# Head pairs 4 and 5 of a planned attention and expert kernel: transposes and squares given to TensorE, bias table stored row by row, a buffer of its own for the first expert columns

## The chip, the cores and the metric

One core of one Trainium2 chip runs the whole program. The metric is device microseconds (us) of one execution. The kernel before takes 1083.62 us (median of three runs, 1081.85 to 1084.55). The profile is of a further execution, which took 1084.82 us by the same measure; its span from the first to the last instruction is 1083.0 us.

## The reference

```python
scores = scale * np.matmul(q, k.transpose(0, 1, 3, 2))      # B=4, H=8, S=576, D=64
x = (log1p(|i - j|) / log1p(max(i, 1)))[..., None]          # relative position
bias = np.maximum(x @ w1 + b1, 0.0) @ w2                    # hidden 32, one value per head
attn = softmax(scores + bias)                               # sum + 1e-9 below the line
x = concat_heads(attn @ v)                                  # (2304, 512)
h = np.maximum(np.maximum(x @ mw1, x @ mw2), x @ mw3) @ mwo # 512 -> 768 -> 512
gate = 1 / (1 + np.exp(-(h @ w_gate)))                      # 512 -> 1536
out = (gate * (h @ w_val)) @ w_out                          # 1536 -> 512, fp32
```

## The kernel before

**Numbers as pairs.** Most fp32 factors are split into a high and a low fp16 part, and a product is three fp16 matmuls (`mm3`, L914). The scale of a split comes from a sum of squares, which either ScalarE takes (`square_sum`, L581) or TensorE: five bf16 matmuls of the data with itself and a diagonal sum on VectorE (`square_sum_pe`, L593, L594).

**Attention.** Work goes by head pairs: P = 0 to 15, four to a batch. A pair has five steps, one for each tile of 128 query rows (the last has 64). A step (`pair`) loads its bias rows from the table `bias_d` (L815 on SP's queue or L816 on ACT's), makes the scores on PE (L804, L807), adds the bias with a row minimum on DVE (L820), takes the exponential on ACT (L821) and the reciprocal sum on DVE (L822, L823). The weights then have to be transposed, in one of two ways. `by_pe` scales them in fp32 on POOL (L831) or DVE (L832), transposes nine 128x128 blocks on PE (L836) and copies them out of PSUM (L574 on ACT, L575 on DVE). `by_dma` writes the high part on ACT (L844) and the low part on DVE (L845) and lets two DMA transposes (L847) move them. `value_out` (L863) multiplies with v: in fp32 (20 matmuls) after `by_pe`, in fp16 (30 matmuls, with v split by `v_hi` and `v_lo`, L785 and L789) after `by_dma`.

All 20 steps of batch 0 (pairs 0 to 3) go `by_pe`, tile by tile over the four pairs, between the rows of the bias table, which are made meanwhile (`bias_rows`, 36 times; each stores 16 table rows of all 8 heads, L661). In batches 1 to 3 the first two tiles of a pair go `by_pe` and the last three `by_dma`. While a pair runs, `prep` loads and splits q, k and v of the pairs to come; the squares of the first four pairs are on PE, those of all later ones on ACT.

**Experts.** `moe1` is the first expert layer of a batch (576 matmuls on L914: 36 column blocks of 12, first all of columns 0 to 255 and then the other 320, three weight matrices in turn for each, then 8 blocks of 18 with the fourth matrix). Its work of batch b-1 is recorded after the first pair of batch b. In batch 0 it keeps six column blocks at a time, three in `hm_f` and three in the end of the tile `X2`, from column 5760 on, and its sums go through two PSUM banks in turn (`mm_b`). The raw words of the fourth weight matrix (`mwo`) pass through two buffers in columns 3072 to 6144 of the same `X2`; their loads and decoding (L674, L536 to L538) are recorded before the first `moe1`. The second layer (`gate`, `outs`) follows at the end; it reuses the attention's memory.

**The planner.** All calls go into a `Recorder`, which notes what reads and writes which memory, and then puts the instructions of all engines into an order (`emit`). Each instruction has a class: BIAS before ATT before MOE before PREP. An engine takes the one that can start first by the planner's own costs, the higher class where two start together, and looks only so far ahead (72 instructions on PE). So the expert layers, class MOE, fill PE wherever the planner sees it idle. A call that has two engines to choose from, such as a copy out of PSUM, goes to the one that would end first. The order is fixed when the program is built; each engine then runs its list strictly in turn.

Of the kernel before, what the change touches and what calls it, by code (L numbers as in the profile page):

```python
# [121 lines left out]
class Recorder:  # L122
# [8 lines left out]
    def __init__(self, nc, untracked):  # L131
        self.nc = nc
        self.untracked = untracked
        self.items, self.first = [], 0
        self.mem = Mem()
        self.cls = 0
        self.joined = None
        self.t_eng = {e: 0.0 for e in self.WINDOW}
        self.busy = {e: 0.0 for e in self.WINDOW}
        self.t_dma = 0.0  # L140
        self.bank = {i: {} for i in range(8)}
        self.log = []
        self.passed = {e: False for e in self.WINDOW}
        for attr, eng in self.ENGINES.items():
            setattr(self, attr, Engine(self, getattr(nc, attr), eng))
# [52 lines left out]
    def cost(eng, method, out, reads, kwargs):  # L198
# [6 lines left out]
        if method.startswith("dma"):  # L205
            if "transpose" in method:
                return 1.33 if n > 1200 else 1.0 + 0.0003 * n, 0.12 + 0.00141 * n, 1.6
            dram = "DRAM" in str(out.space)
            if dram:
                n, parts = 1, 1  # L210
                for _, c in out.ap:
                    n *= c
            size = n * parts * (4 if "32" in str(out.dtype) else 2)
            return (0.45 if eng == "SP" else 0.1), size / (285e3 if dram else 400e3 if size > 6e5 else 300e3) * (1.6 if parts == 64 and n > 500 else 1.0) + 0.03, 1.85
        if eng == "PE":
            f32 = "float32" in str(reads[0].dtype)
            if method == "transpose":
                return 0.045 + 0.00055 * n, 0.0, 0.22
            if n <= 8:
                return 0.142, 0.0, 0.22  # L220
            t = (max(n / 2400, 0.03) + 0.0023) * (4 if f32 else 1)
            if kwargs.get("tile_position") is not None:
                depth = reads[0].ap[0][1]
                t *= (depth if depth < 128 else parts) / 128
                t += 0.012 if f32 else 0.008 if depth < 128 else 0.004
                if n <= 64:
                    t += 0.012
            return t, 0.0, 0.22
# [13 lines left out]
        t = {"tensor_tensor": 0.3 + 0.002 * n, "tensor_scalar": 0.08 + 0.00112 * n, "tensor_copy": 0.08 + 0.00112 * n}.get(method, 0.1 + 0.003 * n)  # L242
# [4 lines left out]
    def start(self, it, e):  # L247

        t = self.t_eng[e]
        for d in it.deps:  # L250
            e2, lat, own = self.ends[d]
            x = own if e2 == e == "PE" else lat
            if x > t:
                t = x
        for i in it.banks:
            for o, x in self.bank[i].items():
                if o != e and x > t:
                    t = x
        return t
# [33 lines left out]
    def emit(self):  # L293
# [15 lines left out]
        while left:  # L309
# [11 lines left out]
            if work:  # L321
                self.t_dma = max(self.t_dma, s + 0.3) + work
                f = self.t_dma + lat
                self.ends[it.k] = (None, f, f)
            else:
                self.ends[it.k] = (e, s + busy + lat, s + busy)
                for i in it.banks:
                    self.bank[i][e] = s + busy + lat
# [8 lines left out]
            stale |= {o for o in lists if self.passed[o] or picks[o] and (len(picks[o][1].alts) > 1 or picks[o][1].banks & it.banks)}  # L337
# [69 lines left out]
SIDE_CLS = ATT  # L407
TI1, T2 = 12, (24, 32, 36, 36, 36)
# [29 lines left out]
def tile_kernel(ctx, tc, q, k, v, w1, b1, w2, mw1, mw2, mw3, mwo, gw, vw, ow, xtab, masks, out):  # L438
# [17 lines left out]
    bias_d = dram.tile([H, S, SB], F32, tag="bias_d", name="bias_d")  # L456
# [46 lines left out]
    e_r = ring(Am, 2, 2 * S)  # L503
    PT0 = take(Am, 2304)
    PT1 = take(Am, 2880)
    pt0 = PT0.rearrange("p (t s) -> p t s", t=9)
    pt1 = [PT1[:, 1440 * e:1440 * (e + 1)].bitcast(F16).rearrange("p (t s) -> p t s", t=9) for e in range(2)]
    rvb0 = PT1[:, 0:2560].rearrange("p (h t d) -> p h t d", h=H, t=NIT)
# [133 lines left out]
    def bias_rows(ti):  # L642
# [18 lines left out]
        nc.sync.dma_start(bias_d[:, 16 * ti:16 * ti + 16, :].rearrange("h i j -> i h j"), bsb[:, 0:SB])  # L661
# [68 lines left out]
    def qk_squares(P, j):  # L730
        if j == 0:
            qs_t[P] = tiny_ap(2)
        (square_sum if P >= PPB else square_sum_pe)(rqk[:, j].rearrange("p h t d -> p (h t d)"), qs_t[P][:, j:j + 1])
# [35 lines left out]
    def v_squares(b, j):  # L769
        if j == 0:  # L770
            vs_t[b] = tiny_ap(PPB)
        (square_sum if b else square_sum_pe)(raw_v(b)[:, 2 * j:2 * j + 2].rearrange("p h t d -> p (h t d)"), vs_t[b][:, j:j + 1])
# [36 lines left out]
    def pair(P, it):  # L809
# [3 lines left out]
        src = bass.AP(tensor=bias_d.tensor, offset=(h0 * S + 128 * it) * SB + 64, ap=[[SB, m], [S * SB - 64, 2], [1, S]])  # L813
# [57 lines left out]
    def prep(u):  # L871
# [3 lines left out]
        if PPB <= P < NP:  # L875
            if P % PPB == 0 and s == 2:
                v_scales(b)
            if s == 5:
                v_hi(P)
            if s == 6:  # L880
                v_lo(P)
        Pl, s2 = divmod(u, 10)
        if 0 <= Pl < NP - PPB and s2 == 8:
# [45 lines left out]
    def moe1(b, xd, mm):  # L929
# [28 lines left out]
        if b == 0:  # L958
            mm_0 = [mm, mm]
            hms = [t[:, 320 * i:320 * (i + 1)] for t in (hm_f, X2[:, 5760:6912]) for i in range(3)]  # L960
# [87 lines left out]
    for b in range(1, B):  # L1048
        for P in range(PPB * b, PPB * b + PPB):
            for it in range(NIT):  # L1050
                m, (e, r) = rows[it], pair(P, it)
                if it < 2:
                    by_pe(e, r, m, pt0[:, :, 128 * it:128 * it + m])
                else:
# [8 lines left out]
            value_out(P, 256, 320, vb, pt1, False)  # L1063
# [178 lines left out]
```

## Time and profile before

| | |
|---|---|
| three runs, median (lowest to highest) | 1083.62 us (1081.85 to 1084.55) |
| profiled execution, its own time | 1084.82 us |
| its span, first to last instruction | 1083.0 us |
| PE busy / DVE / ACT / POOL | 1019.7 / 635.3 / 552.3 / 130.3 us |
| mean granted TensorE clock | 0.979 |

A page of the profile gives the busy time of each engine (part 1) and the span in 40 slices of 27 us (part 2: tenths of a slice; PEclk in tenths of the full 2.4 GHz). The timeline lists instructions in order, runs of equal ones merged (xN); a row's us reaches to the end of its last matmul, so the pace of a run is read from the start of one row to the start of the next. A bracket at the end of a row is idle time before it and what ended it.

### The profile page before, as it was taken

Reading aid. Unit: us, or ns where it says so; the run is one execution under the profiler, and the core shown is the slowest. Engines: PE = TensorE matmul, PEld = TensorE weight load, DVE = VectorE, ACT = ScalarE, POOL = GpSimd, SP = SyncE. Lnnn points to the kernel's source line nnn. Section 1 sums busy time; section 2 is a strip of 40 time slices with the busy share of each in tenths; the row PEclk is TensorE's granted clock in tenths of the full one; section 3 lists DMA queues with packets and bytes.
Section 4 is the critical chain, followed back from the end, with each engine's and each line's share of the span. In section 5 each row is a group of like instructions: output and inputs, shape, how many; then the busy total and the mean of one; then the engine's idle time right before and its main releaser. Section 6 shows DMA issues by size and latency. Waiting matters only on the chain.

```text
span 1083.0 us, 20927 instructions
## 1 busy us (share of the span) xinstructions
PE 1019.7 (94%) x8232; PEld 685.9 (63%) x8232; DVE 635.3 (59%) x1576; ACT 552.3 (51%) x1159; POOL 130.3 (12%) x159
## 2 busy tenths in 40 slices
PE   5877897799999999999999999999999999999998
PEld 2343465466566666676678777777765666776643
DVE  5866887788787887878899947922221221212210
ACT  6877896678788877777666426522110111211100
POOL 1011223503120422211110000000000000000000
PEclk9989898889999999999999999999999999999999
DMA  7767675978998989969855421000000000000001
GB/s 224 210 202 232 209 221 167 246 162 197 228 232 184 234 220 203 206 136 237 160 162 156 154 81 40 20 2 1 10 11 21 19 10 10 11 11 10 11 20 39
DMA packets 181133, 132.96 MB, mean 123 GB/s; under 512 B 123308, under 2 KB 152236, under 8 KB 181036
## 3 DMA queue, kind: packets, MB, share of 16 engines
q1 hardware_dynamic: 177364, 124.26, 46.0%
q10 hardware_dynamic: 3672, 7.38, 2.3%
q8 instruction: 64, 1.05, 0.4%
q14 instruction: 33, 0.27, 0.1%
HBM read 89.53 MB, written 16.52 MB: 98 GB/s over the span
## 4 chain that ended last, share of the span: by engine, by line
PE 79%; DVE 8%; DMA 6%; ACT 4%; issue 2%; POOL 1%; SPq 0%; ACTq 0%; POOLq 0%; DVEq 0%
PE ps L914 46%; PE ps L1179 13%; PE ps L863 6%; PE ps L804 4%; PE ps L836 4%; PE ps L650 2%; DMA bias_d<-am 2%; PE ps L807 2%; DMA am<-in_q_dram 1%; DVE am L820 1%; ACT am L574 1%; POOL am L831 1%; DMA am<-am 1%; PE ps L548 1%; DVE wm L944 1%
## 5 line engine op out<-in xcount | busy, mean ns | idle before, releaser
L914 PE MATMUL ps<-wm 128*128 128x320 f16 (+2 forms) x2304 | 305.1, 286 | 3.3 <-DVE wm L944 2.9
L914 PEld LDWEIGHTS <-am 128*128 128x128 f16 x2304 | 225.5, 98 | 58.8
L914 PEld LDWEIGHTS <-wm 128*128 128x128 f16 x2304 | 222.8, 99 | 60.3 <-issue 8.8
L914 PE MATMUL ps<-x,am 128*128 128x288 f16 x1728 | 214.3, 286 | 0.0
L821 ACT ACTIVATE am<-am,small 128x576 f32<-128x576 f32 (+1 forms) x160 | 123.0, 770 | 43.9 <-DVE small L820 37.7
L1179 PE MATMUL ps<-wm 128*128 128x512 f16 x648 | 142.0, 379 | 0.0
L1153 DVE SCALAR_TENSOR_TENSOR wm<-ps,wm 128x576 f32<-128x576 f32 x48 | 36.4, 757 | 161.6 <-PE ps L914 160.4
L820 DVE CUSTOM_DVE_ANT_0 am<-ps,am 128x576 f32<-128x576 f32 (+1 forms) x160 | 117.6, 748 | 22.4 <-issue 5.5
L1150 ACT ACTIVATE wm<-ps,ug 128x576 f32<-128x576 f32 x48 | 35.6, 741 | 155.0 <-PE ps L914 154.8
L1179 PEld LDWEIGHTS <-wm 128*128 128x128 f16 x648 | 63.4, 98 | 74.0
L1154 ACT CAST wm<-wm 128x576 f16<-128x576 f32 x48 | 32.2, 671 | 129.4 <-DVE wm L1153 129.4
L863 PE MATMUL ps<-am 128*64 128x320 f16 (+3 forms) x1000 | 88.4, 323 | 6.9 <-DVE small L594 4.5
L831 POOL TENSOR_SCALAR am<-am,small 128x576 f32<-128x576 f32 (+1 forms) x73 | 70.2, 971 | 198.1 <-DVE small L823 118.5
L836 PE MATMUL ps<-ident,am 128*128 128x128 f32 x396 | 66.5, 290 | 11.1 <-POOL am L831 7.5
L914 PE MATMUL ps<-am 128*128 128x288 f16 x576 | 71.2, 286 | 0.0
L574 ACT ACTIVATE am<-ps 128x512 f32<-128x512 f32 (+3 forms) x128 | 58.5, 473 | 15.3 <-PE ps L836 13.8
L1184 DVE TENSOR_TENSOR am<-ps,uo 128x512 f32<-128x512 f32 x16 | 11.1, 692 | 93.3 <-PE ps L1179 93.3
L845 DVE SCALAR_TENSOR_TENSOR am<-am,small 128x576 f16<-128x576 f32 (+1 forms) x72 | 59.2, 847 | 10.3 <-ACT am L844 9.7
L836 PEld LDWEIGHTS ps<-ident,am 128*128 128x128 f32 x396 | 45.7, 146 | 28.2 <-POOL am L831 15.3
L804 PE MATMUL ps<-am 64*128 64x512 f16 (+1 forms) x390 | 57.0, 389 | 3.2 <-DVE small L820 3.1
L581 ACT ACTIVATE junk<-am 128x640 bf16<-128x640 f32 (+1 forms) x72 | 48.8, 678 | 20.2 <-DVE am L538 8.9
L863 PEld LDWEIGHTS ps<-am 128*64 128x64 f32 x640 | 41.9, 150 | 22.7 <-issue 8.9
(148 smaller groups left out, 1181.1 us busy)
## 6 DMA issues: line engine op xcount, KB each, us to landing
am<-bias_d SPq DMA_DIRECT2D x52, 576.0 KB, 4.4
bias_d<-am SPq DMA_DIRECT2D x36, 320.0 KB, 3.5
wm<-in_moe_w_dram SPq DMA_DIRECT2D x12, 768.0 KB, 5.5
am<-bias_d ACTq DMA_DIRECT2D x12, 576.0 KB, 4.4
am<-in_moe_w_gate_dram SPq DMA_DIRECT2D x12, 512.0 KB, 4.6
am<-in_moe_w_val_dram SPq DMA_DIRECT2D x12, 512.0 KB, 4.6
am<-in_moe_w_out_dram SPq DMA_DIRECT2D x12, 512.0 KB, 3.4
out_dram<-am SPq DMA_DIRECT2D x36, 128.0 KB, 2.3
```

The costliest lines, as they stand in the source:

```text
L574: nc.scalar.activation(dst, src, AF.Copy, scale=scale)
L581: nc.scalar.activation(junk[:, 0:n], src, AF.Square, accum_out=acc)
L804: nc.tensor.matmul(s_main[o][:m], lhsT=q_[h, eq], rhs=k_[h, ek, 0:512], start=(i == 0), stop=(i == 2), tile_position=(64 * o, 0))
L820: nc.vector.tensor_tensor_reduce(e[:m, c], S_[o][:m], bt[:m, c], -1.0, 3.0e38, ALU.add, ALU.min, mx[:m])
L821: nc.scalar.activation(e[:m, c], e[:m, c], AF.Exp, scale=-1.0, bias=mx[:m], accum_out=l[:m, o:o + 1])
L831: nc.gpsimd.tensor_scalar(e[:m, c], e[:m, c], r[:m, o:o + 1], 1.0, op0=ALU.mult, op1=ALU.mult)
L836: nc.tensor.transpose(ps[:, t], e[:, 128 * (t0 + t):128 * (t0 + t) + 128], ident)
L845: nc.vector.scalar_tensor_tensor(ph[:m, 1, c], e[:m, c], f, ph[:m, 0, c], op0=ALU.mult, op1=ALU.subtract)
L863: nc.tensor.matmul(ps[64 * o:64 * o + 64, :N], lhsT=vv[:, o, tv], rhs=pp[:, tb], start=(i == j == 0), stop=(i == len(todo) - 1 and j == 4) ...
L914: nc.tensor.matmul(ps, lhsT=W(wp, kk), rhs=X(xp, kk), start=(first and i == 0), stop=(last and i == 2))
L1153: nc.vector.scalar_tensor_tensor(hm3(sg), pv, DOWN2, hm3(sg), op0=ALU.mult, op1=ALU.mult)
L1179: nc.tensor.matmul(po, lhsT=gT[:, gi, kk, 128 * ct:128 * ct + 128], rhs=OW[:, wi, kk], start=(kk == 0 and i == 0), stop=(kk == K2 - 1 and ...
```

## The change

1. **Pairs 4 and 5 whole by PE** (`PE_ALL = 6`). Their tiles 2, 3 and 4 go `by_pe` into an fp32 view of the same memory (`pt1_f`), and their second `value_out` is in fp32 from the raw v. `v_hi` and `v_lo` fall away for them, and the loads of the next batch's v into the same places come two substeps later (`prep`).
2. **Squares of batch 1 on PE** (`PE_SQ = 8`): q and k of pairs 4 to 7 and v of batch 1, twelve in all, through the PSUM region `sq_w`.
3. **The bias table as [row, head, column]** instead of [head, row, column]. A store of 16 rows is then one piece of DRAM, and a load reads 128 pieces of 4608 bytes (two heads side by side) instead of 256 of 2304.
4. **A buffer of its own** (`hm_x`, 960 columns of `Am`) for the three expert column blocks of batch 0 that were in `X2`.
5. **The planner's costs**: dearer DMA transposes, DMA issues on SP, POOL scalings and tiled matmuls; and a DMA may not be placed before the one eight places earlier has landed (`lanes`).

```diff
@@ class Recorder
+        self.lanes = [0.0] * 8
...
-                return 1.33 if n > 1200 else 1.0 + 0.0003 * n, 0.12 + 0.00141 * n, 1.6
+                return (1.55 if n > 1200 else 1.1 + 0.0003 * n), 0.12 + 0.00141 * n, 1.6
...
-        t = {"tensor_tensor": 0.3 + 0.002 * n, "tensor_scalar": 0.08 + 0.00112 * n, ...
+        t = {"tensor_tensor": 0.3 + 0.002 * n, "tensor_scalar": 0.09 + 0.0014 * n, ...
...
+        if it.alts[e][1][1]:
+            t = max(t, self.lanes[0])
...
+                self.lanes = self.lanes[1:] + [f]
@@ tables and buffers
+PE_ALL, PE_SQ = 6, 8
-    bias_d = dram.tile([H, S, SB], F32, tag="bias_d", name="bias_d")
+    bias_d = dram.tile([S, H, SB], F32, tag="bias_d", name="bias_d")
+    hm_x = take(Am, 960)
+    pt1_f = PT1.rearrange("p (t s) -> p t s", t=9)
@@ bias_rows
-        nc.sync.dma_start(bias_d[:, 16 * ti:16 * ti + 16, :].rearrange("h i j -> i h j"), bsb[:, 0:SB])
+        nc.sync.dma_start(bias_d[16 * ti:16 * ti + 16].rearrange("i h j -> (i h) j"), bsb[:, 0:SB])
@@ qk_squares (v_squares alike, with PPB * b + j < PE_SQ)
-        (square_sum if P >= PPB else square_sum_pe)(rqk[:, j].rearrange("p h t d -> p (h t d)"), qs_t[P][:, j:j + 1])
+        x, acc = rqk[:, j].rearrange("p h t d -> p (h t d)"), qs_t[P][:, j:j + 1]
+        if P < PE_SQ:
+            square_sum_pe(x, acc, sq_w if P >= PPB else sq_q)
+        else:
+            square_sum(x, acc)
@@ pair
-        src = bass.AP(tensor=bias_d.tensor, offset=(h0 * S + 128 * it) * SB + 64, ap=[[SB, m], [S * SB - 64, 2], [1, S]])
+        src = bass.AP(tensor=bias_d.tensor, offset=(128 * it * H + h0) * SB + 64, ap=[[H * SB, m], [SB - 64, 2], [1, S]])
@@ prep
-            if s == 5:
+            if s == 5 and P >= PE_ALL:
                 v_hi(P)
-            if s == 6:
+            if s == 6 and P >= PE_ALL:
                 v_lo(P)
         Pl, s2 = divmod(u, 10)
-        if 0 <= Pl < NP - PPB and s2 == 8:
+        if s2 == 0 and PPB <= Pl - 1 < PE_ALL:
+            Pl -= 1
+        elif s2 != 8 or PPB <= Pl < PE_ALL:
+            Pl = NP
+        if Pl < NP - PPB:
             load_v(Pl // PPB + 1, Pl % PPB)
@@ moe1
-            hms = [t[:, 320 * i:320 * (i + 1)] for t in (hm_f, X2[:, 5760:6912]) for i in range(3)]
+            hms = [t[:, 320 * i:320 * (i + 1)] for t in (hm_f, hm_x) for i in range(3)]
@@ batches 1 to 3
                 if it < 2:
                     by_pe(e, r, m, pt0[:, :, 128 * it:128 * it + m])
+                elif P < PE_ALL:
+                    by_pe(e, r, m, pt1_f[:, :, 128 * (it - 2):128 * (it - 2) + m])
                 else:
                     by_dma(e, r, m, pt1, 128 * (it - 2))
...
-            value_out(P, 256, 320, vb, pt1, False)
+            value_out(P, 256, 320, vb, pt1_f if P < PE_ALL else pt1, P < PE_ALL)
```

The changed program's line numbers are higher: L574 becomes L581, L581 becomes L588, L593 L600, L815 L830, L820 L835, L821 L836, L831 L846, L832 L847, L836 L851, L847 L862, L863 L878, L868 and L869 L883 and L884, L914 L933, L944 L963.

**ACT in batch 0.** ACT's list of before, in the fourth tile of batch 0: exponentials (L821), copies of transposes (L574 am<-ps), weight splits (L684) and squares of batch 1 (L581 on am 128x640).

```order
L684 ACTIVATE wm<-wm,small 128x768
L821 ACTIVATE am,small<-am,small 128x576
L868 ACTIVATE wm<-ps,small 128x128
L821 ACTIVATE am,small<-am,small 128x576
L581 ACTIVATE junk,small<-am 128x640
L574 ACTIVATE am<-ps 128x512
L581 ACTIVATE junk,small<-am 128x640
L821 ACTIVATE am,small<-am,small 128x576
```

The same tile in ACT's list of the changed program; L581 on am<-ps,small 128x256 is the copy of a finished expert column block into `hm_x`.

```order
L581 ACTIVATE am<-ps 128x128
L581 ACTIVATE am<-ps 128x512
L581 ACTIVATE am<-ps,small 128x256
L836 ACTIVATE am,small<-am,small 128x576
L691 ACTIVATE wm<-wm,small 128x768
L581 ACTIVATE am<-ps 128x512
L883 ACTIVATE wm<-ps,small 128x128
L581 ACTIVATE am<-ps 128x128
L836 ACTIVATE am,small<-am,small 128x576
L581 ACTIVATE am<-ps 128x512
L581 ACTIVATE am<-ps,small 128x256
```

The squares are gone from this place, and copies of expert blocks stand between the exponentials of batch 0. In the list of before the next such copies come 50 rows further on, in the first pair of batch 1 (x_71 is the tile `X2`):

```order
L581 ACTIVATE junk,small<-am 128x640
L574 ACTIVATE am<-ps 128x4x128
L574 ACTIVATE x_71<-ps,small 128x256 x2
L844 ACTIVATE am<-am,small 128x576
L581 ACTIVATE junk,small<-x_71 128x768
```

There the two copies into `X2` stand behind a square of q and among the squares of the fourth weight matrix.

**DVE at the end of batch 0.** The changed program's list in the fifth tile of batch 0 (L963 takes the maximum with an expert column block, L884 on 128x64 is a value product of that tile, L692 splits the third weight matrix); in the list of before the first L944 after this tile stands 30 rows later, in pair 4.

```order
L963 SCALAR_TENSOR_TENSOR wm<-ps,small,wm 128x256
L692 SCALAR_TENSOR_TENSOR wm<-wm,small 128x768 x2
L963 SCALAR_TENSOR_TENSOR am<-ps,small,am 128x256
L692 SCALAR_TENSOR_TENSOR wm<-wm,small 128x768
L884 SCALAR_TENSOR_TENSOR wm<-ps,small,wm 128x64
```

So the second of the three expert matrices is worked on before batch 0 is over.

**SP in pair 4.** SP's list of before (L847 transposes weights, L764 q and k of a later pair):

```order
L815 DMA am<-bias_d 128x2x576 x2
L847 DMA_TRANSPOSE am<-am 128x9x128
L815 DMA am<-bias_d 128x2x576
L847 DMA_TRANSPOSE am<-am 128x9x128
L847 DMA_TRANSPOSE am<-am 128x9x64 x2
L815 DMA am<-bias_d 128x2x576
```

and of the changed program, at the same place:

```order
L775 DMA_TRANSPOSE am<-am 128x10x128
L830 DMA am<-bias_d 128x1152 x2
L714 DMA am<-in_q_dram 128x2x256
L716 DMA am<-in_q_dram 64x2x64
L775 DMA_TRANSPOSE am<-am 128x10x128
L731 DMA am<-in_v_dram 128x2x256
```

Between the bias loads of these pairs stand only loads and the transposes of q and k; the first L862 comes in pair 6.

## Rows read from the trace of the kernel before

**Rows 1.** The page: busy time, then PE in 40 slices

```profile
PE 1019.7 (94%) x8232; PEld 685.9 (63%) x8232; DVE 635.3 (59%) x1576; ACT 552.3 (51%) x1159; POOL 130.3 (12%) x159
...
PE   5877897799999999999999999999999999999998
```

**Rows 2.** Windows: stretch, length, busy us of each engine, PEclk, DMA, GB/s

```profile
0.00:160.00 160.00, 125.79 (x1273) 66.00 (x1275) 114.87 (x304) 122.92 (x251) 26.14 (x39) 0.94 0.73 218
...
140.00:160.00 20.00, 19.96 (x225) 13.38 (x226) 17.08 (x46) 17.88 (x43) 4.73 (x5) 1.00 0.74 241
...
160.00:226.00 66.00, 50.00 (x406) 31.00 (x402) 51.44 (x144) 43.58 (x109) 25.08 (x25) 0.82 0.68 179
226.00:540.00 314.00, 308.08 (x2672) 210.90 (x2670) 255.59 (x664) 239.87 (x537) 71.22 (x90) 1.00 0.92 205
540.00:672.00 132.00, 129.46 (x1070) 102.20 (x1070) 106.45 (x273) 70.72 (x152) 7.89 (x5) 1.00 0.39 119
```

**Rows 3.** Timeline of PE where the expert matmuls stop and start again

```profile
157.43 0.51 PE L593 MATMUL ps<-wm 128*128 128x128 bf16 x6
157.77 1.14 PE L914 MATMUL ps<-wm 128*128 128x256 f16 x9
...
162.16 0.49 PE L914 MATMUL ps<-wm 128*128 128x256 f16 x3
...
226.05 1.48 PE L914 MATMUL ps<-wm 128*128 128x256 f16 x12
...
227.51 7.69 PE L914 MATMUL ps<-wm 128*128 128x256 f16 x69
...
236.59 9.01 PE L914 MATMUL ps<-wm 128*128 128x256 f16 x78
```

**Rows 4.** Timelines of DVE and ACT at 219 to 221 us

```profile
219.18 1.80 DVE L538 SCALAR_TENSOR_TENSOR x<-x 128x768 int32<-128x768 int32 x2
...
218.89 0.74 ACT L581 ACTIVATE junk<-am 128x640 bf16<-128x640 f32 x1 [1.36 <-DMA am<-in_q_dram]
...
220.15 0.84 ACT L574 ACTIVATE x<-ps,small 128x256 f32<-128x256 f32 x2
```

**Rows 5.** The chain that ended last, 150 to 300 us: start, us, what

```profile
169.86 7.77 DMA wm<-in_moe_w_dram
...
212.40 6.38 DMA am<-in_q_dram
```

**Rows 6.** Timeline of PE in pair 4 and the start of pair 5

```profile
246.56 2.23 PE L863 MATMUL ps<-am 128*64 128x320 f16 x30
248.72 0.77 PE L836 MATMUL ps<-ident,am 128*128 128x128 f32 x5
249.41 0.82 PE L804 MATMUL ps<-am 64*128 64x512 f16 x6
...
257.38 2.38 PE L863 MATMUL ps<-am 128*64 128x256 f32 x20
259.69 0.62 PE L804 MATMUL ps<-am 64*64 64x512 f16 x4
```

**Rows 7.** Groups by line and shape, whole span: busy us, mean ns, idle before

```profile
L831 POOL TENSOR_SCALAR am<-am,small 128x576 f32<-128x576 f32 x66 | 61.2, 936 | 184.5 <-DVE small L823 114.1 <-PE ps L807 30.5 <-ACT am L574 9.7
...
L844 ACT ACTIVATE am<-am,small 128x576 f16<-128x576 f32 x48 | 35.2, 766 | 0.9 <-ACT am L821 0.5 <-DVE small L823 0.4
...
L581 ACT ACTIVATE junk<-am 128x640 bf16<-128x640 f32 x36 | 26.3, 729 | 2.5 <-DMA am<-in_q_dram 1.4 <-DMA am<-in_v_dram 0.8 <-issue 0.2
...
L944 DVE SCALAR_TENSOR_TENSOR wm<-ps,small,wm 128x256 f32<-128x256 f32 x42 | 20.1, 479 | 3.4 <-PE ps L914 2.8
...
L832 DVE TENSOR_SCALAR am<-am,small 128x576 f32<-128x576 f32 x14 | 7.5, 539 | 0.4
```

**Rows 8.** Groups on PE by line and shape, 226 to 640 us

```profile
L836 PE MATMUL ps<-ident,am 128*128 128x128 f32 x198 | 31.4, 278 | 1.1 <-POOL am L831 1.0
```

**Rows 9.** DMA issues of the bias table: KB each, us to landing

```profile
am<-bias_d SPq DMA_DIRECT2D x52, 576.0 KB, 4.4
```

More of the change, by code (lines that the diff above doesn't have):

```diff
@@ L213, in cost @@
             size = n * parts * (4 if "32" in str(out.dtype) else 2)
-            return (0.45 if eng == "SP" else 0.1), size / (285e3 if dram else 400e3 if size > 6e5 else 300e3) * (1.6 if parts == 64 and n > 500 else 1.0) + 0.03, 1.85
+            return (0.55 if eng == "SP" else 0.1), size / (285e3 if dram else 400e3 if size > 6e5 else 300e3) * (1.6 if parts == 64 and n > 500 else 1.0) + 0.03, 1.85
         if eng == "PE":
@@ L224, in cost @@
                 t *= (depth if depth < 128 else parts) / 128
-                t += 0.012 if f32 else 0.008 if depth < 128 else 0.004
+                t += 0.012 if f32 else 0.012 if depth < 128 else 0.006
                 if n <= 64:
@@ L241, in cost @@
             return t + (0.09 if "accum_out" in kwargs and vec else 0.01), 0.0, 0.14
-        t = {"tensor_tensor": 0.3 + 0.002 * n, "tensor_scalar": 0.08 + 0.00112 * n, "tensor_copy": 0.08 + 0.00112 * n}.get(method, 0.1 + 0.003 * n)
+        t = {"tensor_tensor": 0.3 + 0.002 * n, "tensor_scalar": 0.09 + 0.0014 * n, "tensor_copy": 0.09 + 0.0014 * n}.get(method, 0.1 + 0.003 * n)
         if method == "tensor_scalar" and kwargs.get("op1") == ALU.max:
@@ L336, in emit @@
                     stale |= set(u.alts)
-            stale |= {o for o in lists if self.passed[o] or picks[o] and (len(picks[o][1].alts) > 1 or picks[o][1].banks & it.banks)}
+            stale |= {o for o in lists if self.passed[o] or picks[o] and (len(picks[o][1].alts) > 1 or picks[o][1].banks & it.banks or work and picks[o][1].alts[o][1][1])}
             for o, ks in lists.items():
@@ L771, in v_squares @@
             vs_t[b] = tiny_ap(PPB)
-        (square_sum if b else square_sum_pe)(raw_v(b)[:, 2 * j:2 * j + 2].rearrange("p h t d -> p (h t d)"), vs_t[b][:, j:j + 1])
+        x, acc = raw_v(b)[:, 2 * j:2 * j + 2].rearrange("p h t d -> p (h t d)"), vs_t[b][:, j:j + 1]
+        if PPB * b + j < PE_SQ:
+            square_sum_pe(x, acc, sq_w if b else sq_q)
+        else:
+            square_sum(x, acc)
     def v_scales(b):
```

## The prediction

> **What bounds the kernel now.** I read the page first: PE is busy for 1019.7 of 1083.0 us, and its slices read 9 from the tenth on [rows 1]. So the windows come next, cut where PE changes character [rows 2]. From 226 us on PE idles 6 us in 314, then 2.5 in 132, at a clock of 1.00; whatever stands there is paid in PE work, since the expert layer fills what the attention leaves. Before 226 us it is different: 34 us idle up to 160 us, and from 160 to 226 us 16 us idle with a mean clock of 0.82. The clock's two levels are 1.2 and 2.4 GHz, so 0.82 means about 36% of the 66 us at the lower one, 12 us of PE time lost (of which some 9 fell on busy time, busy being 50 of 66). That stretch, the last two tiles of batch 0, is the one place with PE time to win: about 25 us.
>
> Why is it empty, when expert work is there to fill it? The timeline of PE shows L914 stopping at 162.16 us and coming back at 226.05 us, with a run of 69, and then of 78 [rows 3]. In the order of PE 60 matmuls stand before the stop: five blocks of 12 of the first matrix. Blocks four and five must go to the part of `X2` that the raw words of the fourth matrix also pass through. On ACT both copies, `x<-ps,small`, stand at 220.15 us, behind the square of q and just after DVE starts its last two decodes `x<-x` (219.18 us) [rows 4]. From 162 to 220 us the two finished blocks hold the only two PSUM banks that `moe1` has, and no further one can begin. So the stop is a shared buffer, not a lack of work, and not the weights either: the first matrix is used by then, and the copies that PE waits for are not of weights.
>
> **The change part by part.**
>
> *The buffer (gain).* With `hm_x` the copies wait for no decode. I counted L914 in both orders ahead of the 25th step's scores, the last before the return at 226.05 us: 60 before, 252 now. The 192 matmuls that move up cost 192 x 0.115 us = 22.1 us at the pace of [rows 3] (78 in 9.01 us, at full clock). That is below the 25 us the stretch has. But PE, DVE and ACT run strictly in order, and the moved work brings its evacuations: by the orders, DVE gets 18 more maxima and splits ahead of that point at about 0.48 us (L944, [rows 7]), 8.6 us in a stretch where it is busy 51.4 of 66. The attention steps there wait on each other more than on an engine's total, so part of this lengthens the stretch. Bounds: it lengthens by nothing (gain 22 us), or by all of 8.6 us plus as much again for matmuls in front of attention work (gain 5 us). I take 4 us, nearer to the first since DVE has 14.6 us free there and a PE kept busy also runs that stretch's own matmuls at the higher clock: gain 18 us.
>
> *Two pairs by PE (cost).* Six steps, nine transposes each: 54. Five take 0.69 us from the first to the scores behind them [rows 6], 0.138 us each: 7.5 us. Two second value products change form: 30 fp16 matmuls take 2.16 us (246.56 to 248.72), 20 fp32 ones of 256 columns 2.31 us (257.38 to 259.69) [rows 6], so 2.31 x 320/256 = 2.89 us at 320 columns; +0.73 us each, 1.5 us. This lies after 226 us, where PE has no idle time: 9.0 us, all of it paid. In return ACT loses 12 casts of 766 ns and DVE as many subtractions, SP loses 12 transposes, and ACT or DVE get 18 copies out of PSUM; none of these bounds that stretch (DVE 256 and ACT 240 of 314 us [rows 2]), so their balance counts nothing, and it comes to a few us in any case.
>
> *Squares by PE (cost).* Twelve times five matmuls at 0.34 us for six, from 157.43 to 157.77 us [rows 3]: 3.4 us. By the order 35 of the 60 come before the 21st step, where PE has idle time; the other 25 are paid: 1.4 us. ACT loses 12 x (0.73 + 0.19 for reading the sum) us, in a stretch where it is busy three quarters. The wait moves with the square: ACT waited 1.4 us for q and 0.8 us for v over 36 squares [rows 7]. On PE such a wait holds all matmuls behind it, so I count 1 us more. Bounds: 0, and the one long case on the chain, a q load of 6.38 us [rows 5], for several of the twelve.
>
> *The bias table (nothing).* 4.4 us from issue to landing [rows 9] with three buffers ahead. Half as many pieces of twice the length move the same bytes. The trace has no piece of this length at this stride: a load could land 1 us sooner or 2 us later, and up to 226 us the DMA engines are busy about 0.7 of the time [rows 2]. Loads issued a step ahead hide either; if the cover went, DVE would wait at L820 for some of the 20 steps of batch 0. I take 0, with 3 us either way.
>
> *The planner's costs (nothing, with a spread).* POOL's scalings become dearer, and by the orders 25 more go to DVE in all: 539 ns there against 936 on POOL [rows 7], shorter for the step that waits, more work for DVE. Six of them lie before the 17th step. Other DMAs are issued later. After 226 us PE has only 6 us of idle time to lose or win; before 160 us the orders hold the same bias rows and steps in nearly the same place (96 and 116 of 144 bias products before the 7th and the 10th step now, 88 and 120 before). I take 0, with 4 us either way.
>
> The sum: -18 + 9.0 + 1.4 + 1 = -6.6 us against the profiled execution's 1084.8 us (1083.0 of span and 1.8 around it): 1078.2. The median of the runs is 1.2 us below that execution, so 1077.0 us.
>
> The Trainium skill speaks against the second part. Here 198 fp32 transposes ran between 226 and 640 us [rows 8], and the clock from 226 to 540 us was 1.00 [rows 2], with expert matmuls around them. "TensorE: Matmul & The Clock Gate", in "Part 4: PE-mode transpose", says that transposes do not count as activity for the clock in the way that matmuls do. By the rows the sum stays; by the page a pair transposed whole could fall to the lower clock, which is a rival below.
>
> **The rivals.**
>
> *Full recovery.* The stretch does not grow, its own matmuls run at the higher clock, and the start gains a little from ACT's lost squares. For it: from 140 to 160 us, where expert work was there, PE was busy 19.96 of 20 us at a clock of 1.00 [rows 2]. Then -25 + 11.4 and 1 us at the start: 1069 us. Against it: DVE's added work.
>
> *Given back.* The moved matmuls stand in front of attention work one for one and batch 0 ends about 10 us later: -12 + 11.4: 1083 us, no change. For it: steps there hang on single releases of DVE, POOL and PE; against it: 16 of the 66 us PE has nothing to do at all.
>
> *PE stands at the loads (slower).* PE now takes squares of q, k and v of pairs 4 to 7 in its strict order, and q's load waits for the one buffer of the pair before. A load took 6.38 us on the chain, and a weight load 7.77 us [rows 5]. If a third of the twelve squares find their load 4 us away, that is 16 us: -18 + 10.4 + 16 = +8, 1092 us. From 7.6 us of such waits on it is slower than before. Against it: ACT met only 2.2 us in 36, and the planner's `lanes` place DMAs later, so it expects landings later too.
>
> *The lower clock.* Two pairs transposed whole take about ten steps, some 50 us. At the 0.82 of [rows 2] they lose 18%, 9 us: 1086 us. By the page named above this is how it would go; the rows of 226 to 540 us stand against it.
>
> *The change does not do what it says:* the copies into `hm_x` could meet another late buffer. In the order they stand between exponentials of batch 0, so little is left for this; it would leave only the cost, 1095 us, and I put it with the slower case.
>
> **How the numbers follow.** Forecast, around 1077 (1071 to 1082): 0.51. Full recovery: 0.17. Given back: 0.16. PE at the loads, with the buffer that does not help: 0.13. Lower clock: 0.03. A measurement can tell 0.3%, 3.3 us, from no change: faster means under 1080.4, slower over 1086.9. Of the forecast 0.47 is faster and 0.04 the same; full recovery is faster (0.17); given back is the same but for 0.02 on each side; the lower clock and the stalls are slower, less 0.02 that ends as the same. Faster 0.66, same 0.18, slower 0.16. The range of 8 in 10 reaches from the full recovery to just past no change: 1066 to 1087 us.
>
> **What would show it.** The expert matmuls on PE (L933 now) should run on through 160 to 226 us, with copies `am<-ps,small` on ACT there; PE's idle time in that stretch should fall from 16 us to about 6, and its clock rise above 0.9. The scores of the 41st step, the first of batch 2, should stand 5 to 10 us earlier in the span. No DMA transposes of weights until pair 6. L851 should have 450 transposes of the same pace, and PE's busy time after batch 0 should be about 10 us more than what was moved out. I would be wrong in kind if PE shows waits of several us at L600 or at transposes for DMA, if batch 0 ends more than 8 us later, or if the time from the 25th step to the end of batch 3 grows.

## The result and the profile after

The changed kernel takes 1047.19 us (median of four runs, 1041.05 to 1053.29) against 1084.09 us before: 0.9654, interval 0.9581 to 0.9728. Six more runs of it gave 1044.44 us, 0.9637 (0.9609 to 0.9665). That is 37 to 39 us faster; 7 were forecast, and 1047 lies far below the range. The direction was right, the sum was not.

The page of the profiled execution (its own time 1053.29 us, span 1051.5, clock 0.991): busy time, then PE in 40 slices.

```profile
PE 1014.2 (96%) x8326; PEld 687.3 (65%) x8326; DVE 636.0 (60%) x1613; ACT 543.2 (52%) x1142; POOL 114.5 (11%) x141
...
PE   5798998999999899999999999999999999999998
```

Its windows in the columns of [rows 2]:

```profile
0.00:160.00 160.00, 138.07 (x1468) 75.61 (x1469) 134.56 (x362) 135.74 (x277) 26.05 (x38) 0.99 0.77 243
160.00:226.00 66.00, 62.33 (x577) 44.07 (x577) 56.09 (x169) 44.56 (x106) 24.83 (x29) 0.95 0.72 171
226.00:540.00 314.00, 307.50 (x2646) 212.30 (x2644) 261.23 (x691) 234.88 (x534) 60.50 (x74) 0.99 0.93 200
540.00:672.00 132.00, 131.38 (x1078) 104.41 (x1076) 106.00 (x271) 70.84 (x145) 3.15 (x2) 1.00 0.29 91
```

Two stretches changed against [rows 2]. From 160 to 226 us PE is busy 62.3 us where it was 50.0; that was forecast. But it is also busy 138.1 us of the first 160, where it was 125.8, and no term of the sum was about that. By the starts of the scores in PE's timeline the time went in four places:

| stretch | before | after | less by |
|---|---|---|---|
| start to the first step | 29.1 us | 26.0 | 3.1 |
| first to 25th step (batch 0 and pair 4) | 195.6 | 183.0 | 12.6 |
| 25th to 80th step | 300.6 | 290.7 | 9.9 |
| 80th step to the end | 557.7 | 551.8 | 5.9 |

The last two are for the most part work that PE had already done by then: in them its busy time fell by 14.4 of the 15.8 us. PE's idle time in the whole span (span less busy time) fell from 63.3 to 37.3 us, and the mean clock rose from 0.979 to 0.991.

### The profile page after: what moved, and what is told of

It reads as the page before. It is cut to its first block, busy times and chain, and to the rows that moved or that the text cites. A ratio compares the mean times of both kernels' runs of the same rounds, so it can differ in the third digit from the quotient of the medians.

```text
span 1051.5 us, 21090 instructions
## 1 busy us (share of the span) xinstructions
PE 1014.2 (96%) x8326; PEld 687.3 (65%) x8326; DVE 636.0 (60%) x1613; ACT 543.2 (52%) x1142; POOL 114.5 (11%) x141
## 4 chain that ended last, share of the span: by engine, by line
PE 83%; DVE 8%; DMA 4%; ACT 2%; issue 1%; POOL 1%; SPq 0%; DVEq 0%; POOLq 0%; ACTq 0%
PE ps L933 48%; PE ps L1200 13%; PE ps L878 6%; PE ps L819 4%; PE ps L851 4%; PE ps L657 3%; PE ps L822 2%; DMA am<-in_k_dram 2%; DVE am L835 1%; PE ps L600 1%; PE ps L555 1%; DVE am L763 1%; DMA am<-am 1%; DMA am<-in_q_dram 1%; DMA wm<-in_xtab_dram 1%
## 5 line engine op out<-in xcount | busy, mean ns | idle before, releaser
L933 PE MATMUL ps<-wm 128*128 128x320 f16 (+2 forms) x2304 | 312.3, 288 | 0.1
L933 PEld LDWEIGHTS <-am 128*128 128x128 f16 x2304 | 225.5, 98 | 58.8
L933 PEld LDWEIGHTS <-wm 128*128 128x128 f16 x2304 | 224.7, 100 | 59.3 <-issue 6.3
L933 PE MATMUL ps<-x,am 128*128 128x288 f16 x1728 | 214.3, 286 | 0.0
L836 ACT ACTIVATE am<-am,small 128x576 f32<-128x576 f32 (+1 forms) x160 | 123.2, 772 | 27.3 <-DVE small L835 23.2
L835 DVE CUSTOM_DVE_ANT_0 am<-ps,am 128x576 f32<-128x576 f32 (+1 forms) x160 | 117.8, 749 | 23.9 <-issue 11.3
L846 POOL TENSOR_SCALAR am<-am,small 128x576 f32<-128x576 f32 (+1 forms) x60 | 60.8, 1017 | 216.6 <-DVE small L838 116.0
L878 PE MATMUL ps<-am 128*64 128x128 f32 (+4 forms) x980 | 82.1, 315 | 1.0 <-DVE wm L884 0.6
L581 ACT ACTIVATE am<-ps 128x512 f32<-128x512 f32 (+3 forms) x149 | 66.0, 466 | 24.2 <-PE ps L851 22.0
L851 PE MATMUL ps<-ident,am 128*128 128x128 f32 x450 | 71.7, 282 | 4.0 <-POOL am L846 3.1
L933 PE MATMUL ps<-am 128*128 128x288 f16 x576 | 71.2, 286 | 0.0
L851 PEld LDWEIGHTS ps<-ident,am 128*128 128x128 f32 x450 | 50.7, 143 | 19.5 <-POOL am L846 8.9
L819 PE MATMUL ps<-am 64*128 64x512 f16 (+1 forms) x390 | 53.6, 380 | 2.0 <-DMA am<-am 2.0
L1176 DVE TENSOR_TENSOR wm<-wm 128x576 f16<-128x576 f32 x48 | 36.4, 758 | 29.3 <-ACT wm L1175 29.3
L860 DVE SCALAR_TENSOR_TENSOR am<-am,small 128x576 f16<-128x576 f32 (+1 forms) x60 | 48.6, 832 | 7.4 <-ACT am L859 7.2
L878 PEld LDWEIGHTS ps<-am 128*64 128x64 f32 x680 | 40.3, 139 | 17.5 <-issue 3.6
```

Source lines behind the costliest of these rows:

```text
L581: nc.scalar.activation(dst, src, AF.Copy, scale=scale)
L819: nc.tensor.matmul(s_main[o][:m], lhsT=q_[h, eq], rhs=k_[h, ek, 0:512], start=(i == 0), stop=(i == 2), tile_position=(64 * o, 0))
L835: nc.vector.tensor_tensor_reduce(e[:m, c], S_[o][:m], bt[:m, c], -1.0, 3.0e38, ALU.add, ALU.min, mx[:m])
L836: nc.scalar.activation(e[:m, c], e[:m, c], AF.Exp, scale=-1.0, bias=mx[:m], accum_out=l[:m, o:o + 1])
L846: nc.gpsimd.tensor_scalar(e[:m, c], e[:m, c], r[:m, o:o + 1], 1.0, op0=ALU.mult, op1=ALU.mult)
L851: nc.tensor.transpose(ps[:, t], e[:, 128 * (t0 + t):128 * (t0 + t) + 128], ident)
```

## The experiments

Eighteen runs. A name in bold is a label; times are medians, ratios are against the kernel before, run beside each. A profile is of one execution.

**The bias table.** *lay* is the kernel before with the table as [row, head, column] and nothing else; *split* keeps [head, row, column] with all its pieces and strides, and only cuts the table into five DRAM tiles of 128 rows each.

```diff
# lay
-    bias_d = dram.tile([H, S, SB], F32, tag="bias_d", name="bias_d")
+    bias_d = dram.tile([S, H, SB], F32, tag="bias_d", name="bias_d")
...
# split
+    bias_d = [dram.tile([H, min(128, S - 128 * i), SB], F32, tag=f"bias_d{i}", name=f"bias_d{i}") for i in range(5)]
...
```

> The kernel before with the bias table as [row, head, column] and nothing else; the orders of PE, DVE and POOL are word for word those of before, and only waits of SP's queue fall away (a load of the table no longer waits for stores of other rows, nor a store for loads). Theory (waits that are not needed, counted at nothing in the prediction): the waits of SP's stores for bias loads (30 us between 15 and 140 us) and of its loads for stores (21 us) go, the last bias row is made 8 to 18 us earlier, and the time falls by 8 to 18 us. Rival (the earlier start of the changed kernel comes from its planner's costs and from the squares taken off ACT): within 3 us of before.

> The kernel before with its bias table cut into five DRAM tiles, one for each 128 rows; layout, pieces of 2304 bytes and strides inside a tile as before. Waits between loads of one tile of rows and stores of the next can't arise. If the waits are the cause, it gains what the row by row layout gains, within 3 us. If longer pieces of DRAM are the cause, it stays within 3 us of before.

**lay**: 1067.33 us, 0.9843 (0.9805 to 0.988). **split**: 1064.93 us, 0.9819 (0.9785 to 0.9853). So the change that was counted at nothing is worth 16 to 18 us alone, and longer pieces are not the reason, since *split* has the old ones. The order of PE, DVE and POOL in *lay* is that of before word for word. What differs are the waits. Rows 53 and 54 of SP's list, before and then *lay* (DMAHW0 to 7 are counters of landed DMAs, which the program's DMAs take in turn):

```
53 L815 DMA am<-bias_d 128x2x576 [waits DMAHW6_49]
54 L815 DMA am<-bias_d 128x2x576 [waits DMAHW7_49,DMAHW5_49]

53 L815 DMA am<-bias_d 128x1152 [waits DMAHW6_49]
54 L815 DMA am<-bias_d 128x1152 [waits DMAHW7_49]
```

Row 54 of before also waits for the store in row 52 (DMAHW5), which writes other rows of the table. With the head outermost, 16 rows of eight heads and 128 rows of two heads cover address ranges that interleave; with the row outermost, or in another tile, they are apart, and in *lay* and *split* alike this wait is gone. In the trace these are waits of SP's queue, 15 to 140 us (us in total, times, longest). Before:

```profile
SPq L661 <- DMA am<-bias_d: 30.1, 9, 5.0
SPq L815 <- DMA bias_d<-am: 20.7, 8, 3.1
```

*lay*, its longest two, and then *split*, where L662 is the store:

```profile
SPq L661 <- ACT am L574: 37.4, 17, 5.6
SPq L815 <- DVE small L820: 7.1, 4, 2.6
```

```profile
SPq L662 <- ACT am L574: 30.6, 17, 5.8
```

Before, stores waited 30.1 us for loads and loads 20.7 us for stores, in a queue that runs strictly in turn. Now a store waits for the row that it is to store, as it should. The waits of before reached PE over two steps, to be read in the same stretch of before:

```profile
ACT am L574 <- DMA bias_d<-am: 12.3, 6, 3.3
...
PE ps L650 <- ACT am L574: 11.2, 10, 3.5
```

ACT could not write the next bias row because the store of an older one had not gone out, and PE (L650, the bias products) waited for ACT. In *lay* the first row is gone and the second is 1.9 us; its 25th step stands at 201.3 us instead of 224.7. The landing itself got no faster (medians: stores 3.5 us before, 4.6 in *lay*; loads 4.4 and 5.0).

**The buffer.** *hm* is the kernel before with `hm_x` alone; *lay_hm* is *hm* with the table; *a_oldhm* is the changed kernel without the buffer.

```diff
# hm (a_oldhm the other way round)
+    hm_x = take(Am, 960)
-            hms = [t[:, 320 * i:320 * (i + 1)] for t in (hm_f, X2[:, 5760:6912]) for i in range(3)]
+            hms = [t[:, 320 * i:320 * (i + 1)] for t in (hm_f, hm_x) for i in range(3)]
```

> The kernel before with a buffer of its own for the three expert column blocks of batch 0 and nothing else. By the prediction's first term: 192 or so expert matmuls move into 160 to 226 us, PE's idle time there falls from 16 us to 6, and the time falls by 14 to 22 us (no squares and no transposes added, so nothing is paid). Rival (given back): the moved matmuls hold up batch 0, and the time falls by less than 6 us.

> The kernel before with the row by row table and the buffer of its own, and the old planner costs, no pair whole by PE and no further squares there. If the two gains lie in different stretches (before and after 160 us), they add: 25 to 36 us below before, so at or below the changed kernel, which pays some 11 us of PE work besides. If they share the same waiting, it is no better than the better of the two alone by more than 5 us.

> The changed kernel with the three column blocks in X2 again. If the buffer gains only together with the pairs by PE (they use up in batch 1 the PE time that the moved work leaves idle), it is 8 to 16 us slower than the changed kernel, though the buffer alone gained nothing. If the buffer's work is given back whatever batch 1 does, it is within 3 us of the changed kernel.

**hm**: 1082.97 us, 0.9995 (0.997 to 1.0019): nothing. **lay_hm**: 1062.96 us, 0.9802 (0.9771 to 0.9833), 4 us below *lay*, with intervals that overlap. **a_oldhm**: 1066.24 us, 0.9854 (0.9828 to 0.988): within the change, taking the buffer away costs 19 to 22 us (8 to 16 were expected). Windows of *hm* show both why it should help and why it doesn't (from 160 to 226 us before: [rows 2]):

```profile
160.00:226.00 66.00, 60.44 (x594) 44.22 (x591) 55.57 (x155) 46.86 (x116) 24.24 (x25) 0.97 0.60 173
...
300.00:340.00 40.00, 30.51 (x214) 18.12 (x214) 27.06 (x73) 27.80 (x64) 6.98 (x10) 0.79 0.84 196
```

From 160 to 226 us PE gained 10.4 us of busy time and clock, as forecast. From 300 to 340 us it now idles 9.5 us at a clock of 0.79, where before it idled 0.1 us:

```profile
300.00:340.00 40.00, 39.92 (x355) 27.51 (x354) 31.29 (x85) 33.20 (x80) 8.12 (x11) 1.00 0.98 214
```

Taken from score to score the account closes. From the first to the 25th step PE's idle time falls from 36.8 to 26.9 us and the clock rises from 0.90 to 0.96; from the 25th to the 80th the idle time rises from 5.2 to 17.9 us and the clock falls from 1.00 to 0.97. With the clock's loss in us (the stretch times one minus the clock) some 21 us are won in the first and lost in the second. The expert matmuls of before (L914) and of *hm* (L915) from 290 to 340 us (PE and PEld busy, clock, DMA, GB/s) tell why:

```profile
290.00:340.00 50.00, 31.95 (x229) 21.80 (x228) 1.00 1.01 221
```

```profile
290.00:340.00 50.00, 10.82 (x84) 7.82 (x82) 0.83 0.89 200
```

The matmuls that moved up were missing later: batch 0's expert layer has only 576 of them, and the next batch's are recorded after the first pair of batch 2. By the orders of PE 375 expert matmuls stand ahead of the 37th step's scores before, and 552 in *hm*. The holes that stay open are the waits of transposes and scores, in *hm*'s timeline of PE:

```profile
321.18 0.66 PE L837 MATMUL ps<-ident,am 128*128 128x128 f32 x4 [0.56 <-POOL am L832]
...
326.94 1.33 PE L837 MATMUL ps<-ident,am 128*128 128x128 f32 x5 [2.73 <-POOL am L832]
...
332.99 0.58 PE L805 MATMUL ps<-am 64*64 64x512 f16 x1 [0.98 <-DVE small L821]
```

**Pairs and squares.** *a_44* is the changed kernel without either (`PE_ALL, PE_SQ = 4, 4`), *a_pe4* has the squares only (4, 8), *a_sq4* the pairs only (6, 4); *b_pe8_sq4* gives all four pairs of batch 1 to PE (8, 4).

```diff
-PE_ALL, PE_SQ = 6, 8
+PE_ALL, PE_SQ = 4, 4
```

> The changed kernel without the two parts that its title names: no pair whole by PE and no square of batch 1 on PE; table, buffer and costs as changed. If those two parts do nothing for the time together, it lies between 1042 and 1050 us, like the two kernels that lack one of them. If they save something that the other covers for, it is 1055 us or more.

> The changed kernel with pairs 4 and 5 transposed by DMA in their last three tiles again; squares, table, buffer and costs as changed. Theory (the expert work moved up before 226 us is missing in batch 1, whose attention is then bound by its own chain of casts, DMA transposes and evacuations, with PE idle): the two pairs by PE take casts and transposes out of that chain and put PE work where PE was idle, so without them it is 5 to 10 us slower than the changed kernel, and PE's idle time and low clock from 226 to 540 us come back (18 us idle, 0.97, as with the buffer alone). Rival (the prediction: each us of PE work after 226 us is paid): 9 us faster than the changed kernel.

> The changed kernel with the twelve squares of batch 1 on ACT again. By the prediction 2 us faster than the changed kernel (1.4 us of PE work and 1 us of waits at loads gone). Rival (ACT's time is what batch 0 and 1 wait for): 3 to 8 us slower.

> The changed kernel with all four pairs of batch 1 whole by PE and its squares on ACT. If PE still has time to fill in batch 1 (after the buffer's work has moved up), the second two pairs gain as the first two did, 2 to 4 us below the kernel with two pairs and squares on ACT (1042.6 us); if PE's time is full there by now, their 9 us of PE work are paid: 1048 to 1052 us.

**a_44**: 1050.07 us, 0.9692 (0.9665 to 0.9719). **a_pe4**: 1048.78, 0.9691 (0.9663 to 0.9718). **a_sq4**: 1042.59, 0.9631 (0.9605 to 0.9658). **b_pe8_sq4**: 1049.80, 0.9695 (0.9671 to 0.9719). So the squares change the time by -1 us (*a_44* to *a_pe4*) and +2 us (*a_sq4* to *after2*, 1044.44), inside the intervals. Two pairs, whose 9 us of PE work were to be paid, make the kernel 7 us faster where the squares are on ACT, and 2 to 4 us where they are on PE (*a_pe4* against the two measurements of the changed kernel, hardly clear of the intervals). Windows of *a_44* and, behind it, of the second profile of the changed kernel:

```profile
260.00:300.00 40.00, 32.27 (x238) 19.62 (x234) 29.63 (x82) 30.00 (x67) 6.33 (x10) 0.83 0.92 216
```

```profile
260.00:300.00 40.00, 39.89 (x337) 26.28 (x333) 35.20 (x97) 33.68 (x80) 8.52 (x12) 1.00 1.02 231
300.00:340.00 40.00, 40.00 (x364) 27.94 (x363) 34.02 (x85) 34.73 (x78) 9.61 (x11) 1.00 1.00 206
```

Without the pairs, PE runs dry around the start of batch 2 as in *hm*; with them it is full there at a clock of 1.00. Between the scores of the 37th and the 51st step PE's idle time is 1.6 us before, 13.4 in *hm*, 14.3 in *lay_hm*, 10.5 in *a_44*, 9.3 in *a_pe4*, 3.3 in *a_sq4* and 0.1 in that second profile (3.8 in the first). Two more pairs find only those 3.3 us left and are paid: +7 us.

The pairs do not stand in that hole themselves: they are steps 21 to 30. Their PE work holds expert matmuls back, and these fill it. By the orders 585 expert matmuls stand ahead of the 37th step in *a_44*, so the layer of batch 0 is used up there, and 459 in *a_sq4*; from the 37th to the 51st step *a_sq4* then does 276 of them in 73.7 us, where *a_44* does 174 in 73.8. The pairs also lose casts and DMA transposes; no run takes these away alone.

**The planner's costs.** *cost* is the kernel before with all new costs and `lanes`; *lay_cost* and *hm_cost* add the table or the buffer; *a_oldcost* is the changed kernel with all the old ones; *a_olddma* has the old DMA costs and no lanes, *a_oldpool* the old POOL and tiled matmul costs, *a_oldpoolonly* the old POOL cost; *b_pool16* is *a_sq4* with POOL's scaling planned at 1.08 us instead of 0.90.

```diff
# a_oldpoolonly
-        t = {... "tensor_scalar": 0.09 + 0.0014 * n, "tensor_copy": 0.09 + 0.0014 * n} ...
+        t = {... "tensor_scalar": 0.08 + 0.00112 * n, "tensor_copy": 0.08 + 0.00112 * n} ...
# a_olddma
-        if it.alts[e][1][1]:
-            t = max(t, self.lanes[0])
...
```

> The kernel before planned with all the new costs and the lanes, and nothing else. If the costs gain by themselves (fewer transposes on PE that stand waiting for a scaling on POOL: 10.7 us of such idle time with table and buffer at the old costs, 3.3 at the new), 6 to 15 us below before. If they gain only where the buffer lets expert work be placed freely, within 3 us of before.

> The kernel before with the row by row table and the new costs; no buffer of its own, no pair whole by PE, squares on ACT. If each part's gain adds, table 16 and costs 11: 1054 to 1058 us. Then the pairs and squares cost 9 to 11 us where the buffer is missing (1066 us with them), as the prediction had it, and save 6 us where it is there (1050 to 1044 us), since PE then has nothing to do in the stretch around the start of batch 2. If instead it is 1063 us or more, the pairs cost nothing without the buffer either, and the buffer's 22 us come from elsewhere.

> The kernel before with the buffer of its own and the new costs; the old table, no pair whole by PE, squares on ACT. If buffer and costs need each other, 12 to 20 us below before, where the buffer alone gave nothing. If the buffer's work is given back in batch 2 at any costs, no better than the costs alone by more than 3 us.

> The changed kernel planned with the costs of before and without the lanes of DMAs. By the prediction within 4 us of the changed kernel. Rival (the plan fits the chip better with the new costs, so that fewer instructions stand in front of a late DMA): 5 to 12 us slower.

> The changed kernel planned with the old costs of DMA transposes and SP's issues and without the lanes; new costs of POOL and of tiled matmuls. If the planner's view of the DMAs is what the costs bring, it is some 14 us slower than the changed kernel, like the one with all old costs (1061 us); if POOL's costs are, it stays within 4 us.

> The changed kernel planned with the old costs of POOL's scalings and of tiled matmuls; new costs of the DMAs, and the lanes. If POOL's share of the scalings is what the costs bring (25 more of them on DVE, 539 against 936 ns, in steps that wait for each other), it is 8 to 14 us slower than the changed kernel; if the DMAs are, it stays within 4 us.

> The changed kernel planned with the old cost of POOL's scalings alone; tiled matmuls, DMAs and lanes at the new costs. If POOL's cost is what counts, as slow as with both old (1052 us, 8 us over the changed kernel) and with the idle time of PE's transposes behind POOL back at some 7 us; if that of tiled matmuls is, within 3 us of the changed kernel.

> The changed kernel with the squares of batch 1 on ACT and POOL's scalings planned at 1.08 us instead of 0.90 for 576 elements (measured 0.94 to 1.02 us), so that more of them go to DVE. If POOL's optimistic cost still leaves transposes on PE waiting, 2 to 5 us below 1042.6 us; if DVE is the scarcer engine by now, the same or slower.

| run | us | ratio (interval) |
|---|---|---|
| cost | 1072.08 | 0.9906 (0.9882 to 0.993) |
| lay_cost | 1051.09 | 0.9728 (0.9692 to 0.9765) |
| hm_cost | 1070.15 | 0.9879 (0.9857 to 0.99) |
| a_oldcost | 1061.32 | 0.9801 (0.9774 to 0.9829) |
| a_olddma | 1047.32 | 0.9679 (0.9649 to 0.9709) |
| a_oldpool | 1052.17 | 0.9707 (0.9681 to 0.9733) |
| a_oldpoolonly | 1047.62 | 0.9672 (0.9649 to 0.9696) |
| b_pool16 | 1044.28 | 0.9644 (0.9608 to 0.968) |

The costs give 11 us alone (1083.1 to 1072.1), 16 on top of the table (*lay* to *lay_cost*) and 14 to 17 within the change (*a_oldcost* to it): a term of its own, also counted at nothing. With the table they make 32 us by the medians, where 16 and 11 are 27; the intervals don't tell these apart. On top of them the buffer alone brings 2 us (*hm_cost*), and a still dearer POOL nothing (*b_pool16* against *a_sq4*). Two expectations were missed, both on the side of a larger gain: *lay_cost* lies below its 1054 to 1058 us, and *a_oldcost* is 14 to 17 us above the changed kernel, not 5 to 12. Two signs of what the costs do can be read. The first step's scores come at 29.1 us before, 26.3 in *cost*, 28.6 in *a_olddma* and 25.5 in *a_oldpool*, so that part hangs on the DMA costs and lanes. And transposes wait less for POOL; groups of PE in *lay* and in *lay_cost* (L840 is the same line):

```profile
L836 PE MATMUL ps<-ident,am 128*128 128x128 f32 x396 | 65.9, 288 | 11.3 <-POOL am L831 8.9 <-ACT am L574 2.0
```

```profile
L840 PE MATMUL ps<-ident,am 128*128 128x128 f32 x396 | 64.1, 285 | 8.0 <-ACT am L578 4.0 <-POOL am L835 3.6 <-ACT junk L585 0.2
```

8.9 us of waiting for POOL became 3.6, but the waits for ACT doubled, so the transposes' idle time fell by 3.3 us in all. Together these two signs cover some 5 of the 16 us. Most of the time between the two profiles, 9.9 of 15.3 us, goes between the 25th and the 80th step, where PE's idle time is 7.5 us in *lay* (4.0 of it one wait for a square on ACT) and 0.3 in *lay_cost*. The parts put back one by one cost 3 (DMA), 8 (POOL and tiled matmuls) and 3 us (POOL alone) against *after2*; only the 8 is clear of the intervals. That the tiled matmuls are worth the other 5 is a difference inside the intervals, and no run changed them alone. The rest stays open: each cost reorders the whole list.

**The same kernel again, and together.** *after2* is the changed kernel once more, beside the others.

> The changed kernel once more, as the measure for the three beside it. Its four executions so far spread from 1041 to 1053 us, those with the squares on ACT from 1041 to 1043. If the spread comes from squares on PE that stand in front of everything when a load of q or k is late, it spreads again by 6 us or more, with PE idle before L600 in the longer ones; if not, it stays within 4 us.

**after2**: 1044.44 us (above), from 1039.77 to 1047.18: a spread of 7.4 us. Its profile is of the longest of the six, and there PE waits 3.2 us for a load of q before squares of batch 1 (L600), so both signs are there, as far as one profile tells. Yet *b_pool16*, with these squares on ACT, spreads from 1037.18 to 1048.97, so the squares on PE aren't needed for it. With table and costs in all four, buffer against pairs and squares gives:

| | neither pairs nor squares | both |
|---|---|---|
| no buffer | 1051.09 (*lay_cost*) | 1066.24 (*a_oldhm*) |
| buffer | 1050.07 (*a_44*) | 1044.44 (*after2*) |

The buffer is worth 1 us without the pairs and 22 with them; pairs and squares cost 15 us without the buffer and save 6 with it. Neither is a number of its own. Of the 15 us some 10 are PE work by the sum under "Two pairs by PE" below; the rest of the difference between the two profiles is idle time and clock, and no run parts pairs from squares without the buffer. *a_sq4* at 1042.59 is the lowest median, but its interval overlaps that of *after2*; no version here is shown to beat the changed kernel.

## Why the prediction was wrong, point by point

**The bias table** ("nothing", 3 us either way) was the first step that failed: it measured -16 and -18 us. I weighed bytes, pieces and landing [rows 9], and took the loads as hidden because they are issued a step ahead. They were not free to go when they were issued. The trace of before had it in the queue's own waits, 30.1 and 20.7 us, which I did not weigh; and the 34 us that PE idles before 160 us [rows 2] I left without a cause.

**The planner's costs** ("nothing, with a spread", 4 us) failed as well: -11 us alone, -14 to -17 in the change. I counted moved instructions and saw them in nearly the same place; a list that keeps its counts can still lose waits. Which waits make the 16 us is shown only for a part.

**The buffer** (-18 us) had the mechanism right and the ledger wrong. The matmuls run through 160 to 226 us and the clock rises, as forecast. The premise that failed is "whatever stands there is paid in PE work, since the expert layer fills what the attention leaves": PE was full after 226 us because of the very matmuls that I moved away. Alone it measured 0. A smaller slip: 160 to 226 us isn't only the last two tiles of batch 0; the scores of pair 4's first four steps stand there too, from 201.3 us on.

**Two pairs by PE** (+9.0 us, "all of it paid") failed by the same premise. Their size was right: span less idle time less the clock's loss (span times one minus the mean clock) is 997 us before, 996 in *a_44*, and 1004 and 1005 in *a_sq4* and *after2*. Their price was not: with the buffer the expert matmuls that they hold back fill the hole that the moved ones left, and they bring 7 us; without it pairs and squares cost 15.

**The sum of these terms was luck.** Buffer, pairs and squares were to bring 6.6 us together (18 less 11.4), and from *lay_cost* to *after2* they bring 6.7. But the buffer alone brings 1 us there and not 18, and the pairs and squares then save 6 and do not cost 11. What the forecast of 1077 lacks is the table and the costs, both put at nothing.

**The squares** (+1.4 and +1 us): not told from 0 by the runs (-1 and +2 us). The wait exists; a link of the chain of the changed kernel's first profile, the load, and PE's timeline there:

```profile
165.96 7.17 DMA am<-in_q_dram
```

```profile
171.63 0.29 PE L600 MATMUL ps<-am 128*128 128x128 bf16 x2 [1.39 <-DMA am<-in_q_dram]
173.18 0.50 PE L600 MATMUL ps<-am 128*128 128x128 bf16 x3 [1.25 <-DMA am<-in_q_dram]
```

2.6 us, one load late, as in the rival that made it slower, but once and not four times. From 160 to 180 us the clock was 0.83 and PE was busy 17.0 of the 20 us; in the second profile, with 3.2 us of the same wait, 15.9, and in *a_sq4* 20.0. How much of the spread of the changed kernel's runs (1041 to 1053 us against 1041 to 1043 for *a_sq4*) this makes stays open.

**The rivals.** "Given back" is what the buffer does alone, though not by delays one for one: in *hm* the 25th step comes 1.9 us later and not 10, and batch 0's expert layer runs out. "Full recovery" names the nearest time (1069), by a mechanism that isn't the one that brought the rest. The lower clock did not come: from 226 to 540 us it is 0.99, with 450 transposes in the kernel. Over the whole span one takes 282 ns (290 before); from 226 to 640 us it is 280 against the 278 of [rows 8].

```profile
L851 PE MATMUL ps<-ident,am 128*128 128x128 f32 x450 | 71.7, 282 | 4.0 <-POOL am L846 3.1
```

So what the Trainium skill, "TensorE: Matmul & The Clock Gate", "Part 4: PE-mode transpose", says of transposes and the clock cost nothing here, with expert matmuls between the transposes; no run here has a long stretch of transposes alone.

**What was to show it.** L933 runs through 160 to 226 us (205 matmuls against 3), PE's idle time there fell from 16.0 to 3.7 us and the clock is 0.95, all as written. The 41st step was to come 5 to 10 us earlier and came 27 earlier (290.1 us against 317.0): that sign was the first to say that something else was at work. L851 has its 450 transposes, and the time from the 25th step to the 80th, the last of batch 3, fell by 9.9 us and did not grow.

## What to carry to other kernels

Read the DMA queue's own waits before its bytes: a load that waits for a store to other rows of the same DRAM table is a wait that the data doesn't need, and here cutting the table or putting the row outermost removed it without a change in the work. Work that fills holes is lent, not given: before counting a moved filler as gain, count what is left for the place that it came from, and look for other work to put there. In a planned kernel measure the parts in pairs, since two parts that are worth 1 us and -15 us alone can be worth 7 together.

## What the runs showed beyond that

The row by row table did not land faster, although a load has half as many pieces of twice the length: a median of 5.0 us in *lay* and 4.6 in the changed kernel against 4.4 [rows 9]. *split*, with the old pieces, lands at 5.1 us, so the length of the pieces isn't what makes the difference. The first four runs spread by 1.2% after the change and by 0.6% before it, but that isn't a property of the two programs: in later runs the kernel before spreads by 1.1% (17 runs beside *lay*) and the changed one by 0.7% (*after2*).
